# Room for late crossbar transposes of q in each engine's order, warm-up products from the first microsecond, a later number for lam's broadcast, and a new table of offsets

One core of one Trainium2 chip. The metric is the device time of one execution, in microseconds.

## The reference, cut to what matters

```python
kv  = np.einsum('bhsd,bhse->bhde', k, v)          # batch 8, heads 8, seq 576, head_dim 64
out = np.einsum('bhsd,bhde->bhse', q, kv)
x   = out / sqrt(mean(out*out, -1) + 1e-6) * g_norm     # then (b, s, 512)
a1  = alpha1 * x + beta1
u   = x + lam * einsum('ts,bsd->btd', w_tok, a1)
a2  = alpha2 * u + beta2
out = u + lam * (maximum(a2 @ w_ch1, 0) @ w_ch2)        # 512 -> 2048 -> 512
```

## The kernel before

The kernel records every operation with the engines that may run it and a cost. A list scheduler in its own text then plays a model of the chip forward, and gives each engine a fixed order of instructions. Only the order is used on the chip; there semaphores decide the time. So a constant of the model, or a number in the table of offsets `ORDER`, changes nothing but orders, and how many warm-up products stand in them (31 before).

A few words used below: a warm-up product multiplies constants and its result is not used; the array (TensorE's) is called cold while its granted clock is half, and it cools when the clock falls to half; a bank is one of the eight slices of PSUM that the kernel writes products to; lc, qt, xtl, kvc and a2t are buffers of the kernel.

```python
self.cold = 8.0            # until then the model takes TensorE for half speed
self.late = 2.0            # loads (kinds L and S) land this much later after 30 us
...
o.end = clock[0] + 2.0 + (self.late if o.kind in ("L", "S") and clock[0] > 30 else 0)
...
# whenever the model's TensorE is idle before the first hidden-layer product: a warm-up product
free["PE"] = o.start + (0.43 if t < self.cold else 0.217)
```

From batch 2 on, q is split into two bf16 halves, transposed by crossbar DMA, and added together again. The addition competes for VectorE with everything else:

```python
P.op({"SP": 2.4}, ... e.dma_start(qhlt[...], qhl[...], transpose=True), dma_us=1.5, pri=pri)
for c in range(4):
    P.op({"DVE": ..., "POOL": ...}, ... tensor_tensor(out=qt[...], in0=qhlt[:, 0, c], in1=qhlt[:, 1, c]))  # L757
...
P.op({"DVE": dve_us(n)}, ... tensor_tensor(out=lc, in0=t.flat()[:, 0:n], in1=lam_bc))   # L1197, frees a bank
```

The start: two broadcasts by a product with a row of ones (one row of the array in use), and the warm-up product on a constant `hot`:

```python
for j, dst, key in ((1, e1, "e1"), (0, lam_bc[:], "lam")):
    P.op({"PE": 0.9}, ... e.matmul(t.flat(), ones, vrow[:, j, :]), pri=-990, kind="T", keep=3)   # L1302
P.warm_deps = [P.lastw["hot"][0]]
```

Of the kernel before, what the change touches and what calls it, by code (L numbers as in the profile page):

```python
# [16 lines left out]
S = 576  # L17
# [6 lines left out]
class Op:  # L24
# [4 lines left out]
    def __init__(self, cost, fn, pri, idx):  # L29
        self.cost, self.fn, self.pri, self.idx = cost, fn, pri, idx  # L30
        self.deps, self.raw = set(), set()
        self.alloc, self.tiles = [], []
        self.start = self.end = self.pos = self.eng = None
        self.waits, self.inc, self.lat, self.clock, self.sem = [], False, None, None, None
        self.succ, self.left, self.ready, self.kind, self.keep, self.soft = [], 0, 0.0, None, 0, set()
        self.port, self.tag = False, ""
# [14 lines left out]
class Prog:  # L51
# [5 lines left out]
    def __init__(self, nc, stack):  # L57
        self.nc, self.stack = nc, stack
        self.ops, self.lastw, self.readers = [], {}, {}
        self.ps = stack.enter_context(nc.psum_tensor("ps", [128, 8, 512], F32))  # L60
        self.eng = {"PE": nc.tensor, "ACT": nc.scalar, "DVE": nc.vector,
                    "POOL": nc.gpsimd, "SP": nc.sync, "AQ": nc.scalar}
        self.warm = None
        self.tag = ""
        self.slack = 0.4
        self.window = 6.0
        self.cold = 8.0
        self.late = 2.0

    def ptile(self, n):  # L70
        return PTile(self, n)
# [52 lines left out]
    def schedule(self):  # L124
# [11 lines left out]
        t = 0.0  # L136

        rings = {"HW": [], "SW": []}
        clock = [3.4]

        def flow(to):
            while clock[0] < to - 1e-9:
                busy = [r for r in rings.values() if r]
                if not busy:
                    clock[0] = to
                    return
                step = min(min(r[0][1] for r in busy) * len(busy), to - clock[0])
                clock[0] += step
                for r in busy:
                    r[0][1] -= step / len(busy)  # L150
                    if r[0][1] <= 1e-9:
                        o = r.pop(0)[0]
                        o.end = clock[0] + 2.0 + (self.late if o.kind in ("L", "S") and clock[0] > 30 else 0)
                        heapq.heappush(ends, (o.end, o.idx, o))
                        heapq.heappush(events, o.end)

# [118 lines left out]
        while left:  # L275
            progressed = True
            while progressed:
                progressed = False
                for e in engines:
                    if free[e] > t + 1e-9:  # L280
                        continue
                    o = choose(e)
# [43 lines left out]
            if self.warm is not None and free["PE"] <= t + 1e-9 and t > 0.5:  # L326
                o = self.dummy(t, owner)
# [10 lines left out]
            t = heapq.heappop(events) if events and (due is None or events[0] <= due) else due  # L338
            flow(t)
            while ends and ends[0][0] <= t + 1e-9:  # L340
                _, _, o = heapq.heappop(ends)
# [105 lines left out]

def group(o):

    if o.kind in ("M", "L"):  # L450
        return None
    return "%s %s %.2f" % (o.tag, "".join(e[0] for e in sorted(o.cost)), min(o.cost.values()))
ORDER = {
    'load.0 D 1.20': 98.3,
    'load.0 DP 0.25': -59.3,
    'load.1 P 0.93': -45.3,
    'norm.1 A 0.30': 52.2,
    'norm.2 D 0.69': -41.3,
    'norm.2 DP 0.69': -42.1,
    'norm.3 D 0.20': -1.9,  # L460
    'norm.6 DP 0.69': 64.6,
    'round_in.4 AD 0.69': -10.2,
    'sums.01 DP 0.25': -7.1,
    'sums.01 P 0.11': 72.7,
    'tok.01 P 0.12': -135.1,
    'x.01 D 0.43': -15.5,
    'x.01 D 0.69': -13.6,
    'x.01 DP 0.43': -70.5,
}


# [2 lines left out]
def dve_us(n, mode=1):  # L474
    return 0.16 + n / 960.0 / mode
# [16 lines left out]
def bass_transnormer_attn__then__resmlp_affine_kernel(  # L492
# [15 lines left out]
    with ExitStack() as stack:  # L508
        P = Prog(nc, stack)
# [4 lines left out]
        def sb(name, shape, dt):  # L514
            return stack.enter_context(nc.sbuf_tensor(name, shape, dt))
# [34 lines left out]
        wt = sb("wt", [128, 5, TP], BF16)  # L550
        w1 = sb("w1", [128, 4, FF], BF16)
# [3 lines left out]
        VK = [("x", 1, j) for j in range(4)]  # L555
# [7 lines left out]
        ones = w2f[0:1, 768:896]  # L563
# [6 lines left out]
        def flat(ap):  # L570
            return ap.rearrange("p h d -> p (h d)")
# [12 lines left out]
        qhl = st[:, NS - 2].bitcast(BF16).rearrange("p (x c m) -> p x c m", x=2, c=4)  # L584
        qhlt = st[:, NS - 1].bitcast(BF16).rearrange("p (x c r t) -> p x c r t", x=2, c=4, r=4)
# [150 lines left out]
        def qtr(b, pri):  # L736
            P.tag = "qtr.%d" % b
            def group(c):
                t = P.ptile(1)
                for pr in range(4):  # L740
                    mm_f(t, pr, ["identr"] + ([("qr", c, pr // 2)] if c < 4 else [("qrt", 0), ("qrt", 1)]),
                         lambda pr=pr: flat(qr[:, c, 2 * pr:2 * pr + 2, :] if c < 4
                                            else qrt[:, 2 * pr:2 * pr + 2, :]),
                         lambda: identr[:], pri=pri, keep=3 if b == 1 else 2, after=[("qt", c)])
                dst = qt[:, :, 128 * c:128 * c + 128] if c < 4 else qtt[:]
                P.op({"ACT": act_us(512), "DVE": dve_us(512)}, lambda e, m: copy_to(
                    e, m, dst, t.flat().rearrange("p (r x) -> p r x", r=4)),
                    r=[t], w=[("qt", c)], pri=pri - 5)
            if b >= XQ:
                for c in (0, 2):  # L750
                    for y in range(2):
                        P.op({"SP": 2.4}, lambda e, _, c=c, y=y: e.dma_start(
                            qhlt[:, y, c:c + 2].rearrange("p c r t -> p (c r) t"),
                            qhl[:, y, c:c + 2].rearrange("p c m -> p (c m)"), transpose=True),
                            r=[("qhl", y, c)], w=[("qhlt", y, c)], dma_us=1.5, pri=pri)
                for c in range(4):
                    P.op({"DVE": dve_us(512), "POOL": pool_us(512)}, lambda e, _, c=c: e.tensor_tensor(  # L757
                        out=qt[:, :, 128 * c:128 * c + 128], in0=qhlt[:, 0, c], in1=qhlt[:, 1, c], op=ALU.add),
                        r=[("qhlt", y, c - c % 2) for y in range(2)], w=[("qt", c)], pri=pri - 5, port=True)
                if b % 2 == 0:  # L760
                    group(4)
                return
            for c in range(5 if b % 2 == 0 or b == 1 else 4):
                group(c)
# [461 lines left out]
        for j, src in enumerate((moe_lam, moe_alpha1)):  # L1226
# [4 lines left out]
            pri=-1099)  # L1231
        for j, src in enumerate((moe_lam, moe_beta1)):
            P.op({"AQ": 0.3}, lambda e, _, j=j, s=src: e.dma_start(
                yn[64:97, j, :], s.rearrange("(o d) -> o d", o=1).to_broadcast([33, DM])),
                w=[("yn", j)], dma_us=0.1, pri=-1098)
        for j, src in enumerate((moe_alpha2, moe_beta2)):
            P.op({"AQ": 0.3}, lambda e, _, j=j, s=src: e.dma_start(
                vcol[4 * j:4 * j + 4, :], s.rearrange("(j p) -> j p", p=128)), w=[("vcol", j)],
                dma_us=0.1, pri=-1097)
# [4 lines left out]
        for c0, c1 in ((4, 5), (0, 2), (2, 4)):  # L1244
            o = P.op({"POOL": 0.9}, lambda e, _, c0=c0, c1=c1: e.dma_start(
                wbf2[:, 0:S] if c0 == 4 else wbf[:, c0:c1, 0:S],
                moe_w_tok[512:576, :] if c0 == 4 else
                moe_w_tok[0:512, :].rearrange("(p c) s -> p c s", c=4)[:, c0:c1, :]),
                w=[("wbf", c) for c in range(c0, c1)], dma_us=0.5 if c0 == 4 else 1.6, pri=-800 + c0 % 4, kind="S")
# [4 lines left out]
        D = {"DVE": 0.3}  # L1254
# [4 lines left out]
             w=[("sm", 3)], pri=-999)  # L1259
# [9 lines left out]
             pri=-999)  # L1269
        P.op(D, lambda e, _: e.tensor_copy(out=identr[:], in_=ident[:]), r=["ident"], w=["identr"],  # L1270
             pri=-999)
        P.op(D, lambda e, _: e.memset(ones, 1.0), w=["ones"], pri=-999)
        for n, d in (("k", krt), ("v", vrt)):
            for i in range(2):
                P.op({"DVE": 0.6}, lambda e, _, d=d, i=i: e.memset(d[64:128, i].bitcast(F32), 0.0),
                     w=[(n + "rtz", i)], pri=-999 + 400 * i)
# [3 lines left out]
        for i in range(2):  # L1280
            for h in range(2):
                P.op(G, lambda e, _, i=i, h=h: e.memset(
                    sel0[64 * h:64 * h + 64, i, 2 * i + h:2 * i + h + 1], 1.0), r=["sel0"], w=["sel0"],
                    pri=-998)
# [3 lines left out]
        def warm_fn(e, tile):  # L1288
# [10 lines left out]
            r=[VK[0], VK[1]], w=[VK[1]], pri=-1000)  # L1299
        for j, dst, key in ((1, e1, "e1"), (0, lam_bc[:], "lam")):  # L1300
            t = P.ptile(1)
            P.op({"PE": 0.9}, lambda e, _, t=t, j=j: e.matmul(  # L1302
                t.flat(), ones, vrow[:, j, :], start=True, stop=True),
                r=["ones", VK[j]], w=[t], pri=-990, kind="T", keep=3)
            P.op({"ACT": act_us(512), "DVE": dve_us(512)}, lambda e, m, t=t, d=dst: copy_to(
                e, m, d, t.flat()), r=[t], w=[key], pri=-991)

        E2 = [("yn", 0), ("yn", 1)]
        P.op({"POOL": 1.3}, lambda e, _: e.tensor_tensor(
# [1 line left out]
            r=E2, w=[("yn", 0)], pri=-700)  # L1311
        P.op({"DVE": 0.15, "POOL": 0.35}, lambda e, _: e.tensor_scalar(
            out=wsm[:, 0:1], in0=ident[:, 65:66], scalar1=-1.0, scalar2=None, op0=ALU.mult),
            r=["ident"], w=["neg"], pri=-700, port=True)
        P.op({"DVE": 0.15, "POOL": 0.35}, lambda e, _: e.tensor_tensor(
            out=wsm[:, 1:2], in0=ident[:, 64:65], in1=ident[:, 65:66], op=ALU.add),
            r=["ident"], w=["msk"], pri=-700, port=True)
        P.op({"DVE": 0.15, "POOL": 0.35}, lambda e, _: e.tensor_tensor(
            out=wsm[:, 1:2], in0=wsm[:, 1:2], in1=ident[:, 96:97], op=ALU.add),
            r=["ident", "msk"], w=["msk"], pri=-700, port=True)  # L1320
# [5 lines left out]
            r=[("yn", 0), "e2h"], w=["rrow"], pri=-700)  # L1326
# [5 lines left out]
             r=["ident", ("vcol", 0), ("vcol", 1)], w=[t8], pri=-300, kind="T")  # L1332
        P.op({"DVE": 0.2}, lambda e, _: e.tensor_copy(out=cols[:], in_=t8.flat()[:, 0:8]), r=[t8],
             w=["cols"], pri=-300)
# [94 lines left out]
            ch2(b, B + 40, 55)  # L1429

        P.by_path(P.main0, -500)
        for o in P.ops:
            if o.pri < -500 and o.tag[-2:] == "00" and o.tag[:3] != "tok":
                o.pri -= 3 if "PE" not in o.cost else 0
            if o.pri < -550 and o.tag == "tok.01":
                o.pri = -485
            if o.pri < -500 and o.tag == "wt":
                o.pri -= 4
            if o.pri < -500 and o.tag in ("kv.01", "qtr.01", "sums.01"):
                o.pri -= 6  # L1440
# [33 lines left out]
```

## Time and profile before

| | before |
|---|---|
| median of the first three runs (lowest to highest) | 357.55 us (356.39 to 358.81) |
| span of the profiled run | 356.3 us |
| first k^T v product (L864) | 13.29 us |
| first hidden-layer product (L1161) | 41.03 us |
| from that one to the start of the last product | 312.1 us |

### The profile page before, as it was taken

Reading aid. Unit: us, or ns where it says so; the run is one execution under the profiler, and the core shown is the slowest. Engines: PE = TensorE matmul, PEld = TensorE weight load, DVE = VectorE, ACT = ScalarE, POOL = GpSimd, SP = SyncE. Lnnn points to the kernel's source line nnn. Section 1 sums busy time; section 2 is a strip of 40 time slices with the busy share of each in tenths; the row PEclk is TensorE's granted clock in tenths of the full one; section 3 lists DMA queues with packets and bytes.
Section 4 is the critical chain, followed back from the end, with each engine's and each line's share of the span. In section 5 each row is a group of like instructions: output and inputs, shape, how many; then the busy total and the mean of one; then the engine's idle time right before and its main releaser. Section 6 shows DMA issues by size and latency. Waiting matters only on the chain.

```text
span 356.3 us, 5357 instructions
## 1 busy us (share of the span) xinstructions
PE 345.1 (97%) x2107; PEld 207.9 (58%) x2107; DVE 233.0 (65%) x413; ACT 141.2 (40%) x255; POOL 149.0 (42%) x144
## 2 busy tenths in 40 slices
PE   3999999999999999999999999699999999999996
PEld 1588764567764546557754544457764544457644
DVE  7467686876799898856875886556866583720044
ACT  2454575127712383327620473115750265006500
POOL 2966446036174392358204790028442561140000
PEclk9999999999999999999999999989999999999999
DMA  5899999799921699439921389829922120410022
GB/s 173 251 234 293 207 210 346 133 156 282 261 65 59 172 267 211 106 102 305 197 59 59 117 233 204 135 69 250 265 63 74 59 63 0 93 71 29 2 59 88
DMA packets 90949, 53.62 MB, mean 150 GB/s; under 512 B 56864, under 2 KB 86376, under 8 KB 90924
## 3 DMA queue, kind: packets, MB, share of 16 engines
q1 hardware_dynamic: 60176, 30.81, 37.0%
q0 software_dynamic: 30496, 22.29, 32.3%
q8 instruction: 16, 0.26, 0.3%
q10 hardware_dynamic: 252, 0.18, 0.2%
q14 instruction: 9, 0.07, 0.1%
HBM read 38.20 MB, written 9.44 MB: 134 GB/s over the span
## 4 chain that ended last, share of the span: by engine, by line
PE 94%; DVE 2%; DMA 2%; issue 1%
PE ps L1161 36%; PE ps L1189 35%; PE ps L1054 8%; PE ps L683 3%; PE ps L1289 2%; DMA st<-st 2%; PE ps L692 2%; PE ps L992 2%; PE ps L1067 1%; PE ps L1302 1%; PE ps L961 1%; PE ps L864 1%; PE ps L1346 1%; PE ps L892 1%; DVE qt L757 1%
## 5 line engine op out<-in xcount | busy, mean ns | idle before, releaser
L1189 PE MATMUL ps<-w,ht 128*128 128x512 bf16 (+2 forms) x592 | 141.3, 379 | 0.0
L1161 PE MATMUL ps<-a2t,w 128*128 128x320 bf16 (+1 forms) x768 | 134.0, 327 | 0.0
L1161 PEld LDWEIGHTS ps<-a2t,w 128*128 128x128 bf16 x768 | 73.8, 98 | 46.2 <-DVE a2t L1105 1.0
L1146 ACT ACTIVATE ht<-ps 128x640 bf16<-128x640 f32 (+1 forms) x108 | 70.3, 653 | 60.9 <-PE ps L1161 59.9
L1189 PEld LDWEIGHTS ps<-w,ht 128*128 128x128 bf16 x592 | 56.3, 98 | 59.9 <-issue 2.4
L1207 POOL TENSOR_TENSOR xm<-xm,lc 128x512 f32<-128x512 f32 x28 | 37.1, 1325 | 103.3 <-DVE lc L1197 103.1
L1197 DVE TENSOR_TENSOR lc<-ps,lam_bc 128x512 f32<-128x512 f32 (+2 forms) x37 | 24.9, 672 | 50.1 <-PE ps L1189 48.0
L814 POOL TENSOR_TENSOR xm<-yn,g_bc 128x512 f32<-128x512 f32 x28 | 40.9, 1459 | 31.4 <-DVE yn L809 30.4
L796 ACT ACTIVATE sq<-ps 128x512 f32<-128x512 f32 (+1 forms) x35 | 20.8, 593 | 44.4 <-PE ps L683 44.1
L683 PE MATMUL ps<-kvc,qt 128*128 128x128 f32 x112 | 33.1, 386 | 0.0
L1054 PE MATMUL ps<-rt,wt 128*128 128x512 bf16 x112 | 30.5, 382 | 0.0
L798 DVE TENSOR_REDUCE small<-sq 128x8 f32<-128x512 f32 (+1 forms) x35 | 23.6, 676 | 10.2 <-ACT sq L796 9.9
L692 PE MATMUL ps<-vr,kr 128*128 128x128 f32 x112 | 29.9, 381 | 0.0
L1059 DVE TENSOR_TENSOR xm<-ps,xm 128x512 f32<-128x512 f32 x28 | 19.3, 690 | 15.1 <-PE ps L1054 14.4
L809 DVE TENSOR_TENSOR yn<-ps,small 128x512 f32<-128x512 f32 (+1 forms) x35 | 24.0, 688 | 0.8
L488 ACT ACTIVATE ub<-xm 128x512 bf16<-128x512 f32 (+1 forms) x19 | 10.7, 572 | 32.8 <-DVE xm L1059 32.0
L683 PEld LDWEIGHTS ps<-kvc,qt 128*128 128x128 f32 x112 | 22.4, 200 | 1.8 <-issue 0.2
L692 PEld LDWEIGHTS ps<-vr,kr 128*128 128x128 f32 x112 | 21.5, 200 | 0.7 <-issue 0.2
L757 DVE TENSOR_TENSOR qt<-st 128x512 fp32r<-128x512 bf16 x20 | 16.9, 879 | 7.2 <-DMA st<-st 7.1
L811 DVE TENSOR_TENSOR rt<-yn,ge 128x512 bf16<-128x512 f32 x25 | 20.9, 844 | 0.4
L1147 DVE TENSOR_SCALAR ht<-ps 128x512 bf16<-128x512 f32 (+1 forms) x20 | 14.8, 738 | 7.9 <-PE ps L1161 7.7
L1054 PEld LDWEIGHTS ps<-rt,wt 128*128 128x128 bf16 x112 | 10.9, 98 | 11.8
(155 smaller groups left out, 357.3 us busy)
## 6 DMA issues: line engine op xcount, KB each, us to landing
out_dram<-xm SPq DMA_DIRECT2D x31, 256.0 KB, 2.5
kr<-in_k_dram POOLq DMA_DIRECT2D x7, 1024.0 KB, 8.9
vr<-in_v_dram POOLq DMA_DIRECT2D x7, 1024.0 KB, 11.1
st<-in_q_dram SPq DMA_DIRECT2D x7, 1024.0 KB, 7.7
w<-in_moe_w_ch_dram POOLq DMA_DIRECT2D x8, 512.0 KB, 16.5
st<-in_k_dram SPq DMA_DIRECT2D x2, 512.0 KB, 7.2
st<-in_v_dram SPq DMA_DIRECT2D x2, 512.0 KB, 7.6
st<-in_q_dram SPq DMA_DIRECT2D x2, 512.0 KB, 8.7
```

The lines of the kernel that those rows point to most:

```text
L683: P.op(F, lambda e, _: e.matmul(t.flat()[:, 128 * pr:128 * pr + 128], a(), m(), start=True, stop=True), r=r, w=[t], kind="F", **kw)
L692: P.op(cost, lambda e, _, h=h, c=c: e.matmul(t.flat()[:, 128 * (h - h0):128 * (h - h0) + 128], flat(kr[:, s, h, c:c + 2, :]), flat(vr[:, s ...
L798: P.op({"DVE": dve_us(512)}, lambda e, _: e.tensor_reduce(out=small[rows, s4], in_=sq[rows, s2], axis=AX.X, op=ALU.add), r=[("sq", s2)], w ...
L809: P.op({"DVE": dve_us(512)}, lambda e, _: e.tensor_tensor(out=hview(yn[rows, s3, :]), in0=hview(t.flat(rows)), in1=bc, op=ALU.mult), r=[t, ...
L811: P.op({"DVE": dve_us(512), "POOL": pool_us(512)}, lambda e, _: e.tensor_tensor(out=rto, in0=yn[rows, s3, :], in1=ge1[rows, :], op=ALU.mul ...
L814: P.op({"POOL": pool_us(512)}, lambda e, _: e.tensor_tensor(out=hview(x), in0=hview(yn[rows, s3, :]), in1=g_bc[rows, None, :].to_broadcast ...
L1054: P.op({"PE": 0.216}, lambda e, _, sc=sc: e.matmul(t.flat(), wt[:, sc, 128 * c:128 * c + 128], rt[:, sc, :] if sc < 4 else rtt[:], start=( ...
L1146: return e.activation(dst, src(), ACT.Relu)
L1161: return e.matmul(o, w1[:, dj, 128 * fj:128 * fj + 128], m, start=(dj == 0), stop=(dj == 3))
L1189: P.op({"PE": 0.004 + n * 0.212 / 512}, lambda e, _: e.matmul(t.flat()[:, 0:n], ht[:, fj, 128 * c:128 * c + 128], w2[:, fj, lo:hi], start= ...
L1197: o = P.op({"DVE": dve_us(n)}, lambda e, _: e.tensor_tensor(out=lc[:, lo:hi], in0=t.flat()[:, 0:n], in1=lam_bc[:, lo:hi], op=ALU.mult), r= ...
L1207: lambda e, _: e.tensor_tensor(out=x, in0=x, in1=lc[:, lo:hi], op=ALU.add),
```

## The change

Its intent: the model should expect q's transposes 5 us later, so that no engine stands before them; the array should be taken for cold until 12 us; warm-up products should start at once; and lam's broadcast should not delay the first k^T v. The table of offsets was then searched anew.

```diff
-        self.cold = 8.0
-        self.late = 2.0
+        self.cold = 12.0
+        self.late = {"L": 2.0, "S": 2.0, "Q": 5.0}
...
-  o.end = clock[0] + 2.0 + (self.late if o.kind in ("L", "S") and clock[0] > 30 else 0)
+  o.end = clock[0] + 2.0 + (self.late.get(o.kind, 0) if clock[0] > 30 else 0)
...
-    if o.kind in ("M", "L"):
+    if o.kind in ("M", "L") or o.pri < -9000:
...  ORDER: 15 entries replaced by 21 (among them 'w1.3 P 0.93': -5.8, 'qtr.4 DP 0.69': -34.3)
-                            r=[("qhl", y, c)], w=[("qhlt", y, c)], dma_us=1.5, pri=pri)
+                            r=[("qhl", y, c)], w=[("qhlt", y, c)], dma_us=1.5, pri=pri, kind="Q")
...
-                r=["ones", VK[j]], w=[t], pri=-990, kind="T", keep=3)
+                r=["ones", VK[j]], w=[t], pri=-990 if j else -450, kind="T", keep=3)
-                e, m, d, t.flat()), r=[t], w=[key], pri=-991)
+                e, m, d, t.flat()), r=[t], w=[key], pri=-991 if j else -450)
...
+        P.warm_deps[0].pri = -9999
```

More of the change, by code (lines that the diff above doesn't have):

```diff
@@ L453 @@
 ORDER = {
-    'load.0 D 1.20': 98.3,
-    'load.0 DP 0.25': -59.3,
-    'load.1 P 0.93': -45.3,
-    'norm.1 A 0.30': 52.2,
-    'norm.2 D 0.69': -41.3,
-    'norm.2 DP 0.69': -42.1,
-    'norm.3 D 0.20': -1.9,
-    'norm.6 DP 0.69': 64.6,
-    'round_in.4 AD 0.69': -10.2,
-    'sums.01 DP 0.25': -7.1,
-    'sums.01 P 0.11': 72.7,
-    'tok.01 P 0.12': -135.1,
-    'x.01 D 0.43': -15.5,
-    'x.01 D 0.69': -13.6,
-    'x.01 DP 0.43': -70.5,
+    'ch1.0 AD 0.62': 58.4,
+    'ch2.1 S 0.45': -1.4,
+    'norm.1 D 0.69': 53.4,
+    'norm.1 P 0.07': 22.6,
+    'norm.2 D 0.69': -31.4,
+    'norm.5 D 0.69': -65.9,
+    'norm.5 P 1.33': -5.6,
+    'norm.6 DP 0.69': 56.8,
+    'norm.6 P 1.33': 57.3,
+    'qtr.1 P 0.07': -5.1,
+    'qtr.4 DP 0.69': -34.3,
+    'round_in.4 DP 1.23': -28.1,
+    'round_in.5 DP 1.23': -37.9,
+    'sums.01 P 0.11': 52.5,
+    'tok.01 P 0.12': -17.8,
+    'tok.4 D 0.69': 35.8,
+    'tok.5 P 0.22': -10.7,
+    'w1.0 P 0.93': 6.2,
+    'w1.3 P 0.93': -5.8,
+    'wt P 0.03': -1.5,
+    'x.01 DP 0.43': -6.1,
 }
```

## The prediction

> **What bounds the kernel now.** I read the page first, then the list of waits for TensorE alone, then the timelines around each wait, then the table of stretches for the clock.
>
> ```profile
> PE 345.1 (97%) x2107; PEld 207.9 (58%) x2107; DVE 233.0 (65%) x413; ACT 141.2 (40%) x255; POOL 149.0 (42%) x144
> ...
> PE 94%; DVE 2%; DMA 2%; issue 1%
> ```
>
> TensorE is in use 97% of the span and the chain of waits lies on it for 94%. That alone would say that only fewer products help. The wait list says more: in the whole span TensorE waits twice.
>
> ```profile
> PE ps L1302 <- DVE w L1272: 5.5, 1, 5.5
> PE ps L683 <- DVE lc L1197: 2.8, 1, 2.8
> ```
>
> The first is the launch (the first product, a broadcast of lam, at 5.47 us). The second sits at 228 us, and the timelines of TensorE and VectorE tell what it is:
>
> ```profile
> 227.52 0.39 PE L1189 MATMUL ps<-w,ht 128*128 128x512 bf16 x1
> 230.75 0.33 PE L683 MATMUL ps<-identr,qrt 128*128 128x128 f32 x1 [2.83 <-DVE lc L1197]
> ```
>
> ```profile
> 221.28 0.69 DVE L1059 TENSOR_TENSOR xm<-ps,xm 128x512 f32<-128x512 f32 x1
> 226.38 0.69 DVE L757 TENSOR_TENSOR qt<-st 128x512 fp32r<-128x512 bf16 x1 [4.41 <-DMA st<-st]
> 227.08 0.42 DVE L1074 TENSOR_TENSOR xtl<-ps,xtl 64x256 f32<-64x256 f32 x1
> 227.53 0.69 DVE L757 TENSOR_TENSOR qt<-st 128x512 fp32r<-128x512 bf16 x1
> 228.24 0.43 DVE L1074 TENSOR_TENSOR xtl<-ps,xtl 64x256 f32<-64x256 f32 x1
> 228.69 1.29 DVE L757 TENSOR_TENSOR qt<-st 128x512 fp32r<-128x512 bf16 x2
> 230.00 0.69 DVE L1197 TENSOR_TENSOR lc<-ps,lam_bc 128x512 f32<-128x512 f32 x1
> ```
>
> VectorE stood 4.41 us before an addition of two crossbar-transposed halves of q (L757) that had not landed. The other work, standing behind it in the queue, waited too, among it the multiplication at 230.00 that frees the PSUM bank TensorE needs. What is hidden in the waits shows in the table of stretches (columns: engine busy times, then the granted clock, DMA share, GB/s):
>
> ```profile
> 231.00:232.00 1.00, 1.00 (x7) 0.72 (x6) 0.58 (x2) 0.00 (x0) 1.00 (x1) 0.63 0.61 125
> 232.00:233.00 1.00, 1.00 (x4) 0.39 (x4) 0.33 (x1) 0.49 (x1) 0.04 (x1) 0.50 0.10 28
> 233.00:234.00 1.00, 1.00 (x4) 0.31 (x3) 1.00 (x4) 0.10 (x1) 0.00 (x0) 0.50 0.61 240
> 234.00:235.00 1.00, 1.00 (x5) 0.41 (x4) 0.94 (x3) 0.00 (x0) 0.00 (x0) 0.66 0.00 0
> ```
>
> The pause cooled the array: for 3.4 us the clock is half, and the shortfall is 0.37 + 0.50 + 0.50 + 0.34 = 1.71 us of full-speed time. These two places are one loss of 2.83 + 1.71 = 4.5 us in the profiled run.
>
> The start is the third place. TensorE has no wait from 5.47 us to 227 us, but much of its early work is warm-up products on constants (L1289, 31 of them), which run whether needed or not:
>
> ```profile
> 8.16 1.05 PE L1302 MATMUL ps<-xm,w 1*128 1x512 f32 x1
> 9.14 1.03 PE L1289 MATMUL ps<-hot 128*128 128x512 bf16 x2
> 10.11 0.27 PE L1331 MATMUL ps<-ident,w 8*128 8x8 f32 x1
> 10.31 3.33 PE L1289 MATMUL ps<-hot 128*128 128x512 bf16 x9
> 13.29 0.83 PE L864 MATMUL ps<-vr,kr 128*128 128x256 f32 x4
> ```
>
> ```profile
> 6.42 0.17 DVE L1256 MEMSET hot<- 128x128 bf16 x1
> ...
> 10.59 0.43 DVE L489 CAST vr<-st 128x512 fp32r<-128x512 f32 x1
> ```
>
> The last operand of the first k^T v (L864) is ready at 10.59 + 0.43 = 11.02 us, but the product starts at 13.29: nine warm-up products stood before it, most at 0.42 us each. The kernel orders its instructions by a time model in its own text, which takes the array for cold until 8 us; the spacing falls to 0.216 us only after 12.4 us. So TensorE runs 13.29 - 11.02 = 2.3 us behind, and having no wait later, it carries this up to the first hidden-layer product (L1161) at 41.03 us.
>
> **What the Trainium skill says.** "TensorE: Matmul & The Clock Gate", Part 1 (The HAM clock gate): the array is at half clock until a window of about 3.4 us was busy, falls back after an idle one, and the window is free-running. The trace agrees: half clock for 3.4 us after a pause of 2.83, spacing 0.42 then 0.216 us. It follows that whether a 2.8 us pause cools the array depends on how it lies to the window. "DMA: Bandwidth & Descriptors", Issuing engines are not separate DMA queues: transfers of all issuers share the same 16 DMA engines and interleave. The trace agrees: the 24 q transposes take 2.8 / 6.5 / 12.1 us (min, median, max) from issue to landing. "Perfetto Trace Analysis", Sequencer Loop: an engine instruction waits for its own semaphores in its engine's queue; the 4.41 us before L757 with ready work behind it show that.
>
> **The change, part by part.** No arithmetic is added or removed; the change moves instructions within queues. The model's constants alter its order, and the table of offsets (found by search) is new.
> (a) Transposes of q after 30 us are reckoned to land 5 us later. The four additions L757 should then come after the multiplication that frees the bank. At 228 us they landed at about 226.4; five microseconds behind the model's idea cover the 4.41 us wait. Their reader, the first product of the next normalisation, runs from 235.95 us, and four additions take 4 x 0.69 = 2.8 us, so there is room. Worth 2.83 us of pause, and of the 1.71 us of cold clock what the timed runs have of it. The three runs lie 2.4 us apart (356.39 to 358.81), as if some cooled and some not; I take 1.2 us. I give 85% that no like wait appears elsewhere: 0.85 x (2.83 + 1.2) = 3.4 us.
> (b) The constant of the warm-up products is written first on VectorE (0.17 us, at 0.9 instead of 6.42 us), so they start near 1.1 us. They fill time in which TensorE has nothing. The array may be warm some 3.4 to 7 us later, thus at 4.5 to 8 us instead of 12.4. The single-row broadcasts do not seem to warm it: four of them from 5.47 to 9.14 us left it cold.
> (c) The model takes the array for cold until 12 us, so it plans fewer warm-up products before the first k^T v. If they run faster than planned, TensorE waits for data, which loses nothing.
> (d) lam's broadcast (two of the four L1302 instructions, 3.75 us in all, so 1.87 us cold) moves behind the first k^T v. It is first read by a multiplication at the end of the second layer, far later. This is the same 1.9 us of TensorE time that (b) and (c) also free; it is not added again.
> For (b) to (d) together: k^T v can come 2.3 us earlier. What limits the rest: q's first half is being rounded at 12.20 us (0.63 us) while its transposes start at 14.71, room 1.9 us; w_tok's last piece was issued at 17.33 and took up to 5.5 us, so 22.8, against its first transpose at 24.75, room 1.9 us; the first quarter of w_ch1, issued at 25.86, took 10.9 us, so 36.8, against 41.03, room 4.2 us. The smallest rooms say 1.9 us.
> Sum: 3.4 + 1.9 = 5.3 us. 357.55 - 5.3 = 352.25, say 352.2 us.
>
> **Rivals.** (1) The wait moves. The added order also sets the fourth quarter of w_ch1 ahead of the second. The four landed from 36.8 to 45.0 us, about 2.7 apart, so the second quarter would land third, near 42.3. TensorE gets to it after 10 products at 0.216 and 6 at 0.29 us (how they are spaced now): at 39.1 + 3.9 = 43.0. That is 0.7 us of room; an earlier start than 38.4 turns into a wait for the load. This caps the start gain at some 2.6 us, and against it speaks that the model sees these loads late too. (2) Another place in VectorE's or POOL's queue takes the late wait: 15.1 us of waits for transposes stand on POOL already (2 times), harmless today since outputs alone hang on them. If a bank is held again for 3 us, the gain of (a) is lost and cooling can follow: 355.6. (3) The start is bound by data, not TensorE: the DMA engines are above 90% in most slices from 17 us on, and w_ch1 would not land earlier. Then the start gains nothing: about 354. (4) All goes well: the cold clock counted in full and 2.6 at the start, 2.83 + 1.71 + 2.6 = 7.1, so 350.4.
>
> **Range and chances.** The range runs from rival 4 to a little better than rival 2: 350.0 to 355.0. Two per cent of 357.55 is 7.15 us, so faster means under 350.4, just what the best case gives; some earlier start or a slow draw of the runs before could bring it: 0.17. Slower by 2% needs two new pauses: 0.01. Within: 0.82.
>
> **What would show it.** (a) is right if TensorE's wait for lc is gone, and the clock is 1.00 in every stretch from 20 to 340 us. (b) is right if the first L1289 lies near 1.1 us and spacing is 0.216 before 12. (c, d) are right if the first L864 is at 11.0 to 11.6 and the first L1161 near 39.1 us. From that product to the end there were 315.3 us; without the loss, 310.7. I am wrong if this stretch stays above 313 (a new wait, to be found in TensorE's list), or if L1161 starts at 41 as before (data bound), or if a wait of L1161 for the w loads appears.

## The result, and the profile after

| | before | after |
|---|---|---|
| median (4 runs each, same chip) | 357.0 us | 352.62 us (352.05 to 352.91) |
| ratio, 95% interval | | 0.9867 (0.9826 to 0.9908): within 2% |
| span of the profiled run | 356.3 | 351.1 |
| first k^T v product | 13.29 | 11.03 |
| first hidden-layer product | 41.03 | 40.78 |
| from there to the start of the last product | 312.1 | 307.2 |

A ratio here is the mean time of one kernel's fast runs over that of the other's of the same rounds, so not quite the ratio of the medians quoted.

In the profiled runs nearly all of the gain lies behind 41 us: 312.1 - 307.2 = 4.9 us. The start gave 0.25 us in this pair of runs. Lines L1161, L1189, L757, L1197 and L683 of before are L1167, L1195, L763, L1203 and L689 now (six lines were added). The page, and TensorE's list of waits after:

```profile
PE 344.6 (98%) x2086; PEld 209.3 (60%) x2114; DVE 234.1 (67%) x408; ACT 144.0 (41%) x259; POOL 148.9 (42%) x145
...
PE 96%; DMA 2%; SPq 1%; issue 0%; DVE 0%; ACT 0%
```

```profile
PE ps L870 <- ACT vr L494: 1.4, 1, 1.4
PE ps L1295 <- DVE hot L1262: 1.0, 1, 1.0
PE ps L1195 <- issue: 0.3, 2, 0.2
```

The wait of 2.8 us for lc is gone, and the granted clock is 1.00 in every stretch from 20 us on. VectorE at the same place, after (start, duration, what):

```profile
223.35 0.69 DVE L763 TENSOR_TENSOR qt<-st 128x512 fp32r<-128x512 bf16 x1
224.06 0.42 DVE L1080 TENSOR_TENSOR xtl<-ps,xtl 64x256 f32<-64x256 f32 x1
224.51 0.69 DVE L763 TENSOR_TENSOR qt<-st 128x512 fp32r<-128x512 bf16 x1
...
226.42 0.69 DVE L1203 TENSOR_TENSOR lc<-ps,lam_bc 128x512 f32<-128x512 f32 x1 [0.32 <-PE ps L1195]
227.03 2.35 DVE L763 TENSOR_TENSOR qt<-st 128x512 fp32r<-128x512 bf16 x2
```

No addition waits. Two things differ at once. The additions stand a little later (the first could have started at 222.0 us before, and starts at 223.35 now), and two of them are behind the multiplication. And the third transpose landed at 219.32 us instead of 226.35. GpSimd issued the loads of the next k and v at 202.35 and 205.88 instead of 207.79 and 208.71, and they had landed (at 211.21 and 214.95 us) before the third transpose was issued at 216.22; in the kernel before, that transpose was issued at 218.52, with the load of v in flight until 219.54. Which of the two did it, these two traces cannot tell.

The start is not what I had expected. TensorE's order and the clock in the changed kernel:

```profile
1.04 5.35 PE L1295 MATMUL ps<-hot 128*128 128x512 bf16 x14 [1.04 <-DVE hot L1262]
6.32 1.98 PE L1308 MATMUL ps<-xm,w 1*128 1x512 f32 x4
...
8.49 1.15 PE L1295 MATMUL ps<-hot 128*128 128x512 bf16 x3
11.03 0.80 PE L870 MATMUL ps<-vr,kr 128*128 128x256 f32 x2 [1.39 <-ACT vr L494]
```

```profile
5.00:9.00 4.00, 3.96 (x13) 1.36 (x12) 2.79 (x8) 0.95 (x3) 0.46 (x1) 0.98 0.96 302
9.00:12.00 3.00, 1.61 (x6) 0.86 (x4) 1.17 (x2) 2.11 (x4) 2.81 (x3) 0.50 1.14 294
12.00:16.00 4.00, 4.00 (x18) 3.58 (x16) 1.74 (x4) 2.46 (x6) 2.84 (x4) 0.54 0.91 303
```

Both broadcasts (four L1308 instructions) still stand ahead of k^T v: lam's has a later number now, but it was ready while TensorE had nothing else, so the scheduler took it anyway. And the clock, full at 5.43 us, went back to half from 8.85 to 15.67 us. The array was cold exactly when the first real products came.

### The profile page after: what moved, and what is told of

Read it like the earlier page. It is cut to its first block, busy times and chain, and to the rows that moved or that the text cites. A ratio compares the mean times of both kernels' runs of the same rounds, so it can differ in the third digit from the quotient of the medians.

```text
span 351.1 us, 5353 instructions
## 1 busy us (share of the span) xinstructions
PE 344.6 (98%) x2086; PEld 209.3 (60%) x2114; DVE 234.1 (67%) x408; ACT 144.0 (41%) x259; POOL 148.9 (42%) x145
## 4 chain that ended last, share of the span: by engine, by line
PE 96%; DMA 2%; SPq 1%; issue 0%; DVE 0%; ACT 0%
PE ps L1167 36%; PE ps L1195 36%; PE ps L1060 9%; PE ps L689 4%; PE ps L698 2%; DMA st<-in_v_dram 2%; PE ps L998 2%; PE ps L1295 1%; PE ps L1073 1%; PE ps L870 1%; PE ps L898 1%; PE ps L1352 1%; PE ps L967 1%; PE ps L703 1%; PE ps L945 1%
## 5 line engine op out<-in xcount | busy, mean ns | idle before, releaser
L1195 PE MATMUL ps<-w,ht 128*128 128x512 bf16 (+2 forms) x576 | 134.9, 376 | 0.8 <-issue 0.3
L1167 PE MATMUL ps<-a2t,w 128*128 128x320 bf16 (+1 forms) x760 | 133.8, 327 | 0.3
L1167 PEld LDWEIGHTS ps<-a2t,w 128*128 128x128 bf16 x768 | 73.4, 98 | 44.8 <-DVE ht L1153 0.3
L1152 ACT ACTIVATE ht<-ps 128x640 bf16<-128x640 f32 (+1 forms) x106 | 69.0, 653 | 56.6 <-PE ps L1167 55.5
L1195 PEld LDWEIGHTS ps<-w,ht 128*128 128x128 bf16 x592 | 55.9, 98 | 59.6 <-issue 0.8
L820 POOL TENSOR_TENSOR xm<-yn,g_bc 128x512 f32<-128x512 f32 x28 | 39.5, 1411 | 47.9 <-DVE yn L815 44.8
L1203 DVE TENSOR_TENSOR lc<-ps,lam_bc 128x512 f32<-128x512 f32 (+2 forms) x37 | 25.0, 675 | 48.8 <-PE ps L1195 44.4
L689 PE MATMUL ps<-kvc,qt 128*128 128x128 f32 x112 | 32.5, 381 | 0.0
L804 DVE TENSOR_REDUCE small<-sq 128x8 f32<-128x512 f32 (+1 forms) x35 | 23.6, 676 | 8.4 <-ACT sq L802 8.2
L817 DVE TENSOR_TENSOR rt<-yn,ge 128x512 bf16<-128x512 f32 x27 | 24.4, 912 | 0.4
L689 PEld LDWEIGHTS ps<-kvc,qt 128*128 128x128 f32 x112 | 22.1, 199 | 2.3
L1153 DVE TENSOR_SCALAR ht<-ps 128x512 bf16<-128x512 f32 (+1 forms) x22 | 16.1, 736 | 10.3 <-PE ps L1167 10.2
L494 ACT ACTIVATE ub<-xm 128x512 bf16<-128x512 f32 (+1 forms) x17 | 9.3, 563 | 22.5 <-DVE xm L1065 22.4
L681 DVE TENSOR_TENSOR st<-st 128x1024 bf16<-128x1024 f32 x12 | 16.2, 1367 | 0.2 <-ACT st L494 0.2
```

Of the source, the lines that this page charges most:

```text
L689: P.op(F, lambda e, _: e.matmul(t.flat()[:, 128 * pr:128 * pr + 128], a(), m(), start=True, stop=True), r=r, w=[t], kind="F", **kw)
L804: P.op({"DVE": dve_us(512)}, lambda e, _: e.tensor_reduce(out=small[rows, s4], in_=sq[rows, s2], axis=AX.X, op=ALU.add), r=[("sq", s2)], w ...
L817: P.op({"DVE": dve_us(512), "POOL": pool_us(512)}, lambda e, _: e.tensor_tensor(out=rto, in0=yn[rows, s3, :], in1=ge1[rows, :], op=ALU.mul ...
L820: P.op({"POOL": pool_us(512)}, lambda e, _: e.tensor_tensor(out=hview(x), in0=hview(yn[rows, s3, :]), in1=g_bc[rows, None, :].to_broadcast ...
L1152: return e.activation(dst, src(), ACT.Relu)
L1167: return e.matmul(o, w1[:, dj, 128 * fj:128 * fj + 128], m, start=(dj == 0), stop=(dj == 3))
```

## The experiments

Most of them edit the finished order of one or two engines, after the scheduler has run; the order of all other queues was compared and is the same. An edit that the scheduler answers by ordering everything anew is marked as such. All results were correct. "M" stands for the first hidden-layer product, "stretch" for the time from it to the start of the last product. Each group of four ran on one chip.

**First group: what made the 4.9 us behind M?** Theory: work stands behind an addition that waits (order). Rival: loads collide with the transposes (DMA).

*b_adds_behind*:

```diff
 VectorE, batch 6 (kernel before)
-L757 qt, L1074 xtl, L757 qt, L1074 xtl, L757 qt x2, L1197 lc
+L1074 xtl x2, L1197 lc, L757 qt x4
```

> The kernel before with one edit on VectorE's queue alone: the four additions L757 of the batch that waits at 222 us stand behind the multiplication L1197 that frees the bank; every other queue is the same. If the loss was work standing behind an early wait (my theory), TensorE's 2.8 us wait for lc goes, with it the 3.4 us of half clock, and the time falls by 2.8 to 4.5 us against before: 353 us, ratio about 0.989. If late transposes hurt by another way (bank or a2t still wait), or the gain of the change came from elsewhere, the time stays within 1 us of before, ratio 0.997 to 1.003.

Measured: 358.27 us, ratio 1.0011 (0.9977 to 1.0046). The wait for lc was gone, and TensorE had a new one four microseconds later. First TensorE, then VectorE, of this kernel:

```profile
234.49 0.33 PE L683 MATMUL ps<-kvc,qtt 128*128 128x128 f32 x1 [1.93 <-DVE kvc L718]
```

```profile
232.49 1.51 DVE L1105 TENSOR_SCALAR a2t<-a2t,cols 128x640 bf16<-128x640 bf16 x4 [0.47 <-DMA a2t<-ub]
234.02 0.42 DVE L718 TENSOR_TENSOR kvc<-ps,kvc 64x256 fp32r<-64x256 f32 x1
```

The second half of the k^T v copy (L718) stands behind four instructions that wait for the next transposes (a2t), which are late too, as they follow q's in the same queue. Of the time ahead of L718, 0.5 us is that wait and 1.5 us the four instructions themselves. In the kernel before, the first wait had hidden this one. The stretch took 309.4 us. So the wait I had named was real but not the only one; taking it away alone is worth next to nothing in the timed runs: two of the four cooled (mean 359.2 us), and the two that did not (357.2) are 0.5 us below the mean of before in this group (357.7).

*b_adds_kvc*:

```diff
 VectorE, batch 6 (kernel before)
-L757/L1074 mixed, L1197 lc, L489 kvc, L718 kvc, L1105 a2t x4, L718 kvc
+L1074 xtl x2, L1197 lc, L489 kvc, L718 kvc x2, L757 qt x4, L1105 a2t x4
```

> The kernel before with VectorE's queue alone edited at 222 us: the four additions L757 behind the multiplication L1197 (as in b_adds_behind), and now also the second half of the k^T v copy (L718) ahead of the four a2t instructions that wait for another late transfer. b_adds_behind took the 2.8 us wait away and met a wait of 1.9 us for that L718, which the first had hidden. If these two were all, the stretch from the first hidden-layer product to the last product takes 307.2 to 307.7 us (307.2 in the changed kernel, 312.1 before) and the time is 353.5 to 354.7 us, ratio 0.989 to 0.992. If a third wait follows, the ratio stays over 0.995.

Measured: 354.67 us, ratio 0.9917 (0.9888 to 0.9946), stretch 307.2 us, no wait of TensorE after the launch. VectorE of this kernel, with no bracket (no idle time) before any of them:

```profile
228.43 0.86 DVE L718 TENSOR_TENSOR kvc<-ps,kvc 64x256 fp32r<-64x256 f32 x2
229.32 2.50 DVE L757 TENSOR_TENSOR qt<-st 128x512 fp32r<-128x512 bf16 x4
```

Moving eight instructions (the additions and the a2t four) in one queue of the kernel before gives the whole 4.9 us of the stretch.

*b_loads_early*:

```diff
 GpSimd, batch 6 (kernel before)
+L596 kr load, L596 vr load            (five instructions earlier)
 L814, L811, L1207, L814, L814
-L596 kr load, L596 vr load
```

> The kernel before with one edit on GpSimd's queue alone: the loads of k and v for the same batch are issued five instructions (about 6 us) earlier, as the changed kernel happens to do, so that they should not be in flight together with the four transposes of q. The additions stay where they block VectorE. If transposes were late because of these loads (rival: the change helped by moving loads, not by making room), the third transpose lands near 220 instead of 226.35 us, VectorE's 4.4 us wait is gone and the time falls by 2.8 to 4.5 us, ratio about 0.989. If the lateness has another cause, ratio 0.997 to 1.003.

Measured: 354.71 us, ratio 0.9903 (0.9880 to 0.9926), stretch 307.2 us. The additions stand where they stood, and none waits:

```profile
227.05 0.68 DVE L757 TENSOR_TENSOR qt<-st 128x512 fp32r<-128x512 bf16 x1
230.79 0.69 DVE L1197 TENSOR_TENSOR lc<-ps,lam_bc 128x512 f32<-128x512 f32 x1
```

The third transpose landed at 224.34 us, 2.7 us before the first addition's turn, not after it. (Its profiled run, 358.49 us, was an outlier of the five: TensorE waited 2.0 us for the next batch's q, the array cooled in the start, and M came at 46.4 us, so its times are compared from M on. The other four lie between 353.87 and 354.82. The ratio fits these four; with the outlier the mean is 0.993 of before's.) From M, the loads were issued 159.6 and 160.5 us later instead of 166.8 and 167.7, and the third transpose landed 177.9 instead of 185.3 us later. So the rival holds as well: keeping the loads out of the transposes' way is enough by itself, with the additions left where they were. Lateness and order are both needed for the loss; removing either removes it.

*b_late_q* (ordered anew): `self.late = {"L": 2.0, "S": 2.0, "Q": 5.0}` and `kind="Q"` in the kernel before, nothing else.

> The kernel before with the first part of the change alone, as the change writes it: the ordering model takes transposes of q for 5 us later, everything else (old table, cold until 8 us, warm-up as before) kept. All queues are ordered anew. If this part carries the gain, 353 to 354 us, ratio about 0.990, and the list of TensorE's waits has none over 1 us after the launch. If a new order without its own table brings new waits, 355 to 359 us.

Measured: 354.29 us, ratio 0.9902 (0.9881 to 0.9923), stretch 307.2 us. This constant alone carries the gain behind M. In its order too the loads were issued early (at 203.22 and 205.39 us), and the third transpose landed at 219.13 us.

*a_old_table* (ordered anew): the changed kernel with the `ORDER` of before.

> The changed kernel with the table of offsets of the kernel before. If the model's constants carry the gain, ratio to before 0.985 to 0.992 as the changed kernel has it (0.987). If the table found by search does, it lies at 0.995 to 1.01, with new waits of TensorE of some us in its list.

Measured: 357.98 us, ratio 1.0003 (0.9979 to 1.0026), stretch 311.3 us, with waits of TensorE of 0.8, 0.5 and 0.4 us for ht near 97 and 138 us. These make up a part of the lost 4.1 us only; the rest I did not trace. The constants do not carry the gain with just any table: a new order may bring waits of its own.

**Second and third group: the start.** Theory of the prediction: TensorE lags 2.3 us at the first k^T v, behind planned warm-up products, and carries that lag up to M. Rival: the start is bound by data.

*a_no_early_warm*: the changed kernel without the 14 warm-up products ahead of the first broadcast.

> The changed kernel without its 14 warm-up products ahead of the first broadcast, all else in place. In the changed kernel's trace the clock that they gave was lost again at 8.85 us, before the first k^T v. If the early warm-up is worth nothing (my theory now), the time stays within 0.7 us of the changed kernel, ratio to before 0.985 to 0.990. If it is worth the 1 to 2 us that I predicted, ratio 0.990 to 0.993 and the first hidden-layer product at 42 us or later.

```profile
5.26 3.88 PE L1308 MATMUL ps<-xm,w 1*128 1x512 f32 x4 [5.26 <-DVE w L1278]
...
11.02 0.79 PE L870 MATMUL ps<-vr,kr 128*128 128x256 f32 x2 [0.22 <-ACT vr L494]
```

Measured: 352.58 us, ratio 0.9858 (0.9825 to 0.9890), M at 40.5 us. The early warm-up is worth nothing: the broadcasts, at half speed, still end in time for the data of k^T v.

*b_kvc_fewer_warm*: b_adds_kvc with three instead of nine warm-up products ahead of k^T v.

> The kernel before with VectorE's queue mended as in b_adds_kvc (0.992), and six of the nine warm-up products before the first k^T v taken out; nothing else. The changed kernel has three there. If these planned products alone made TensorE late at the start (my theory for the gain at the start), the first k^T v comes at 11 to 11.6 us instead of 13.3, the first hidden-layer product near 40.5 us instead of 41.5 to 42.5, and the ratio is 0.985 to 0.988, all of what the change gained, without its table. If the gain at the start lies in the table's order, the ratio stays 0.990 to 0.993. If the array now stays cold for longer, it is lost again: 0.990 or more, with half clock until 15 us or later.

Measured: 356.13 us, ratio 0.9957 (0.9904 to 1.0009). k^T v came at 11.2 us, the first token-mixing product at 29.6 instead of 31.0 us, and then TensorE stood still, waiting for ScalarE's rounding of the next batch's q. First TensorE and then ScalarE of this kernel:

```profile
35.30 0.52 PE L683 MATMUL ps<-identr,qr 128*128 128x128 f32 x3 [2.16 <-ACT qr L488]
```

```profile
34.09 2.00 ACT L488 ACTIVATE qr<-st 128x1024 fp32r<-128x1024 f32 x2 [4.92 <-DMA st<-in_q_dram]
```

The lag is removed and nothing is gained by it: in the three runs without a cold window (354.8, 355.1, 355.1 us) it is as fast as b_adds_kvc, and in the other three the pause cooled the array, which cost 2 to 4 us more. So the theory of the prediction falls, and the rival stands: in the order of before, the start is bound by the landing of the next batch's q. The traces agree in a number. In the four runs with this order and a warm array (before, b_adds_behind, b_late_q, b_adds_kvc) q landed at 33.16, 34.48, 33.67 and 33.37 us, and M came 7.9, 8.1, 8.1 and 8.1 us later. In the two that cooled it came 11.1 and 11.3 us later.

*a_strip*: the changed kernel without the 21 warm-up products behind the first k^T v.

> The changed kernel without the 21 warm-up products that stand behind the first k^T v (about 4.6 us of TensorE in all). If planned warm-up products hold real ones back (TensorE waits nowhere from 11 to 348 us in the changed kernel), the first hidden-layer product comes at 38 to 39.7 us instead of 40.8 and the ratio to before is 0.978 to 0.983. If the start is bound by data (landings of w_tok at 23.7, chains over ScalarE and VectorE), TensorE now waits where the products were and nothing is gained: 0.985 to 0.989. If pauses cool the array, worse than that.

Measured: 356.03 us, ratio 0.9949 (0.9911 to 0.9987), M at 43.3 us. The transposes of w_tok started 1.3 us earlier (23.6 us), but the array cooled from 26.52 to 36.76 us, here shown between 30 and 40 us, where w_tok mixes the tokens:

```profile
30.00:40.00 10.00, 10.00 (x66) 8.61 (x65) 5.93 (x14) 4.24 (x8) 3.50 (x4) 0.66 1.39 245
```

Pauses do not explain this: the longest in the 3.41 us before the clock fell was 0.31 us, and TensorE was busy for 3.10 of them, with w_tok's transposes and products of four columns; in the changed kernel full warm-up products stand among these. The warm-up products look like waste in a chain of waits on TensorE, and with them in place the clock stayed up. My expectation of a gain was wrong.

*a_lam_behind*:

```diff
 TensorE (changed kernel)
-L1308 x2, L1337, L1295 x3, L870 x10 (k^T v), L898 ...
+L1308,    L1337, L1295 x3, L870 x10 (k^T v), L1308, L898 ...      and ScalarE's copy of lam likewise
```

> The changed kernel with lam's broadcast really behind the first k^T v: the changed kernel's number for it does not move it, both broadcasts still stand ahead. Only TensorE's and ScalarE's queues change. If single-row broadcasts count as idle for the clock, halving their stretch keeps the array warm (no half clock after 5 to 6 us) and the first k^T v takes 1.2 us instead of 2.9. If the start is bound by later data, the first hidden-layer product still comes at 40 to 41 us and the ratio stays 0.985 to 0.989; if by this early stretch, 39 to 39.5 us and 0.981 to 0.984.

Measured: 358.23 us, ratio 1.0025 (0.9994 to 1.0056), M at 45.8 us. What the change set out to do makes it 5.6 us slower, when it is really done in this order. The broadcast's place became a pause (TensorE waited 1.3, 1.3 and 0.4 us before k^T v), and the array was cold for 13.7 us, although TensorE was busy throughout them; why it took so long to warm, these runs do not show:

```profile
10.00:20.00 10.00, 9.02 (x28) 6.23 (x29) 2.81 (x7) 4.91 (x12) 9.59 (x11) 0.56 0.80 203
20.00:30.00 10.00, 10.00 (x58) 8.55 (x57) 3.88 (x11) 4.58 (x11) 2.14 (x4) 0.75 1.25 298
```

*a_keep_warm*:

```diff
 TensorE (changed kernel)
-L1295 x14, L1308 x2, L1337, L1295 x3
+L1295 x14, L1308, L1295 x6, L1308, L1295 x4, L1337, L1295 x3
```

> The changed kernel with ten more warm-up products, six behind the first broadcast and four behind the second, so that no window of 3.4 us is mostly single-row products. If the array stays warm from 5 to 8 us on, the first k^T v takes 1.2 us instead of 2.7 and, TensorE being busy without a wait up to the first hidden-layer product, that comes up to 1.5 us earlier: 39 to 40 us, ratio to before 0.982 to 0.985. If half the window still counts as idle or data is what bounds, 0.985 to 0.989 as the changed kernel.

Measured: 352.79 us, ratio 0.9870 (0.9827 to 0.9913); the changed kernel in the same rounds (a_same) 0.9861. The clock now holds, in all six runs (0.998 to 1.000, against 0.980 to 0.995 for a_same), and the profile shows 1.00 where the changed kernel had 0.50:

```profile
10.00:20.00 10.00, 10.00 (x65) 7.51 (x64) 4.78 (x12) 7.46 (x17) 9.59 (x10) 1.00 0.86 212
```

But TensorE, ahead of its data, then waits for the next batch's v:

```profile
PE ps L698 <- DMA vr<-in_v_dram: 1.8, 1, 1.8
```

A warm start is worth nothing here, as a landing at 33 to 35 us bounds it.

*a_keep_wtok*: a_keep_warm, and w_tok's loads three GpSimd instructions earlier, released by q's first half.

> a_keep_warm, and the three loads of w_tok three GpSimd instructions earlier, released by the first half of q instead of the second half of k. If the landing of w_tok (23.7 us) is the next bound behind a warm start, this comes out 0.5 to 1.5 us faster than a_keep_warm, 0.979 to 0.983. If not, the same as a_keep_warm; if the loads now hold up v's second half, slower.

Measured: 353.13 us, ratio 0.9886 (0.9839 to 0.9933). w_tok landed at 20.3 instead of 23.0 us and v at 32.8 instead of 35.1. But the loads now stand ahead of GpSimd's rounding of q, for which TensorE waited 1.4 us; the profiled run cooled. The edit brought its own wait, so it says that w_tok's landing is not the only bound, and no more.

*a_same*: the changed kernel again.

> The changed kernel again on the chip of the three others, as their yardstick: ratio to before 0.985 to 0.989. Its single runs should tell how often the clock loses one or two windows (0.995 or 0.990) in the start.

Measured: 352.86 us, ratio 0.9861 (0.9819 to 0.9903). Its profiled run (357.78 us, clock 0.980) was slow and is not compared. Its trace tells one thing: the changed kernel too can stay cold in the start for as long as a_lam_behind did (10.42 to 24.08 us, M at 44.2 us); of its ten runs one did. The five fast runs have a granted clock of 0.989 to 0.995, so one or two cold windows of 3.4 us in each.

No version beat the changed kernel; the one without early warm-up equals it.

## Why the prediction was right, and where it was not

The forecast of 352.2 us met 352.62, and the two terms of its sum, 3.4 us behind M and 1.9 in the start, came out near: the three kernels that mend only the stretch lie at 0.9902, 0.9903 and 0.9917, on average 3.3 us of 357.3, and the three with the changed start at 0.9858, 0.9861 and 0.9867, another 1.6 us (2.1 us between b_adds_kvc and a_no_early_warm, which ran in one group). But the steps behind the terms did not fare alike, and that the start's term met the measured gain is luck: so far as the runs show, none of the steps that led to it was what gave it. By the prediction's own sign, M near 39.1 us and not at 41, it failed in the profiled pair: M came at 40.78 us.

- **The pause and the cold clock are one loss: right.** The stretch shrank by 4.9 us in the profiled pair, against 4.5 worked out, and 310.7 us were forecast for what remained from M to the end; it took 310.3. The 1.2 us put down for the cooling was somewhat high: in the second and third group 9 of 22 runs of before have a clock of 0.995 or so and mean 359.1 us, those at 0.999 to 1.000 mean 356.8, so 0.9 us on average; in the first group none of 7 cooled. Yet b_late_q gained 3.5 us there (0.9902), so the sum was right, but its parts, 2.8 us of pause and the rest cold clock, are those of the profiled run and not of every run.
- **"The four additions L757 should then come after the multiplication that frees the bank": half the story.** They did for two of four. Shown: doing this alone gains nothing (b_adds_behind), because a second wait of 1.9 us lay under the first; with that mended too it gains all (b_adds_kvc); and moving two loads gains as much without it (b_loads_early). I had read the late landing as given. It came in good part from a collision in the same 16 DMA engines, as the section of "DMA: Bandwidth & Descriptors" cited in the prediction would have it, and the order decides on that as well: from M, the third transpose landed 7.4 us earlier in b_loads_early, 3.2 us of it by an earlier issue (174.3 instead of 177.5) and 4.2 by a shorter flight (3.6 instead of 7.8). How late it lands varies: with the loads in their old places it came 182.5 and 182.8 us after M (b_adds_kvc, b_adds_behind), against 185.3 in the profile of before, so not every run need have waited 4.4 us.
- **(b) The early warm-up: wrong.** It starts at 1.04 us as forecast and the clock is full at 5.43, but the broadcasts took it away again before k^T v. Without it the time is the same.
- **(c) Fewer products ahead of k^T v: right as to 11.03 us, wrong as to its worth.** The step that failed is "having no wait later, it carries this up to the first hidden-layer product". A lag that meets no wait is not proof that it delays anything: with the lag gone, a wait of 2.2 us appeared for data that lands at 33 to 34 us (b_kvc_fewer_warm). The rooms that I listed stopped at w_tok and w_ch1; the next batch's q was missing from them, though its wait stands in the list of waits of before (ScalarE waits for q's load; the timeline shows 2.63 us before 33.18 us).
- **(d) lam's broadcast moves: it did not.** I took the description for the fact. A later number does not make this scheduler hold back what is ready while its engine is idle.
- **What gave the 1.6 us in the start** is the order, so far as the traces show: the changed kernel has none of q's transposes (L689) ahead of M, where the kernel before has four (L683), and its first products on the next batch's data need v. M came 6.4 to 7.0 us after v's landing (34.15, 33.48 and 35.07 us in the changed kernel, a_no_early_warm and a_keep_warm), not 8 us after q's. I did not test this by moving those four products alone, so it stays an inference.
- **Rival 3 ("the start is bound by data, not TensorE")** was right that a landing bounds, but named w_ch1, where it was the next batch's q and v, and it was wrong that this leaves no gain. Rival 1 did not come: no product waited for w_ch1. Rival 2, a wait that moves to another place, did not come in the changed kernel, but it is what b_adds_behind met.

## What to carry to other kernels

When a wait is to be removed, look for the next one in the same queue that it hides: here the edit of four instructions gained nothing and that of eight gained everything. A queue without waits may still be late for nothing; ask which landing the next engine would meet if it were early, before counting a lag as a gain. And an idle TensorE costs twice, since a pause of 2 to 3 us brought 3.4 us at half speed in before and 6.8 us in b_kvc_fewer_warm; in a_strip the array cooled with no pause over 0.31 us, amid small products. Filler products can be worth more than the time they take.

## What the Trainium skill lacked or had wrong

- "TensorE: Matmul & The Clock Gate", Part 1, speaks of busy and idle windows and does not say how products that use a small part of the array count. In the changed kernel 2.0 us of one-row products in one window (5.43 to 8.85 us, 3.38 of 3.42 us busy) were followed by 6.8 us at half clock; with six and four full products behind them (a_keep_warm) the clock held at 1.00. In a_strip the clock fell after 3.41 us of which 3.10 were busy, with small products. That such products count less is what these figures suggest; no run separates rows, columns and length.
- The same page gives one idle window of about 3.4 us as the condition for cooling. Here pauses of 2.83 us (before) and 2.2 us (b_kvc_fewer_warm, three of six runs at 0.990 to 0.995) were enough at times: in the 3.41 us before the clock fell, TensorE had still been busy for 0.58 and 1.36 us. So the prediction's "It follows" does not come from the page, by which a pause shorter than the window would not cool.
- "DMA: Bandwidth & Descriptors" has no figure for a crossbar transpose that follows plain loads. Here the third of the same four transposes landed 3.1 us after its issue when the loads of k and v were issued 5.4 and 2.8 us earlier and had landed, and 7.8 us when loads were still in flight (219.32 - 216.22 in after, and 226.35 - 218.52 in before).
